# Two engines in turn for the PSUM copies of the last two softmax chains in an FFT and soft mixture-of-experts kernel

## The chip, the cores and the metric

The kernel runs on one core of one Trainium2 chip. The metric is the device time of one execution in microseconds (us). The engines of a core run side by side, each through its own queue of instructions in order: TensorE (PE in the profile: the matmuls and transposes; PEld: its weight loads), VectorE (DVE), ScalarE (ACT), GpSimd (POOL) and SyncE (SP, which here only issues transfers). TensorE writes its results into PSUM tiles; VectorE or ScalarE copies them from there into SBUF, where TensorE can read them again.

## What is computed

```python
X = np.fft.rfft(x, axis=1)                         # x: 8 x 2496 x 256
y = np.fft.irfft(X * (filt_r + 1j * filt_i)[None], n=2496, axis=1)
x = y.reshape(19968, 256)
logits = x @ phi                                   # 32 slots, 4 for each of 8 experts
d = softmax over the 19968 rows of logits (axis 0)
slot_input = d.T @ x                               # 32 x 256
slot_out[e] = relu(slot_input[e] @ w1[e]) @ w2[e]  # hidden size 1024
c = softmax over the 32 slots of logits (axis 1)
out = c @ slot_out                                 # 19968 x 256
```

## The kernel before

Each of the 8 batches goes through a Fourier transform that is written as two layers of matmuls with a round trip through DRAM between them (`s1_unit`, lines 305 to 312, then `x_unit`, line 339). `x_unit` also multiplies by the filter on VectorE (lines 352 and 353) and adds on VectorE and GpSimd (355, 356). `t_unit` transposes the spectrum (366), copies it to a `y` tile (368), and makes the logits of the spectrum (377, copied to `lt` at 384). One slot of the main loop does one `x_unit` and one `t_unit`; there are ten slots to a batch.

The softmax over the rows needs logits in the time domain. That is done group by group in the generator `chain(g)`. `GROUPS` puts batches 0 and 1, 2 and 3, and 4 and 5 together; group 3 is batch 6 alone, and group 4 is batch 7 alone. The text calls them chain 3 and chain 4: they are "the last two". With one batch in a group, `nb` is 1, `R` is 64 and `SA` is 8, and a chain has these steps. In each, TensorE fills a PSUM tile and one engine copies it:

- `lsb` (transposes at 410): two tiles, of 512 and of 128 columns, copied by VectorE at 411.
- `v1` (matmuls at 423): three tiles of 7, 7 and 6 values of t, copied by ScalarE at 430.
- `v` (transposes at 443): two tiles of 512 and 192 columns, copied by VectorE at 444.
- `lg`, the logits in the time domain (450): two tiles, each read twice, first by a maximum on VectorE (451), then by a copy on ScalarE (457). The maximum over partitions follows in small steps (464, 467, 469, 471, 474, 476).
- `d`: subtract the maximum on VectorE (488), exponential on ScalarE (489), in three pieces.
- `u`, the forward transform of `d` (506): three PSUM tiles of shape [128, 2, 24, 10], that is, 480 floats or 1920 bytes in each partition. Each is copied in two halves, h = 0 and h = 1, by ScalarE at 516: 240 and 240 columns twice, then 180 and 140.
- `u2` (transposes at 523): two tiles of 512 and 128 columns, copied by VectorE at 524.
- `dt` (537): two tiles of 512 and 128 columns, copied by ScalarE at 544.
- `dd` (transposes at 553): two tiles of 512 and 128 columns, copied by VectorE at 554.
- `z` and `s`: the sum and the weighted sum of the rows (561 and 581), added into `s_run` (571 and 591).
- Last the softmax over slots, which only the output needs: `rm` (602), the subtraction (604), the exponential (605), the sum `r_all` (607) and its reciprocal (609, 610).

Chain 3 takes its PSUM tiles from one pool of two; chain 4 takes turns between two such pools, which the other work has left by then.

After the last slot, a loop advances chain 4 and chain 3 in turn until both are done. When they are, the slot inputs are formed (804), the expert network runs (816 to 842) and the output is computed (859 to 912) and written. The weights of the expert network are loaded by SP into buffers as these come free; the last 24 of the 64 weight loads (issued at line 736) go into `y` tiles, which come free when `s` of chain 3, and then `s` of chain 4, has read them, and for four of them when the first layer of the network has read the weights that lie there.

The order in which each engine gets its instructions is not the order of the program text alone. The kernel is built with `schedule_with_timeline_sim=True`: a planner orders the instructions of each engine by a simulated time before the kernel is built, and that order is then fixed. It also sets all waits between engines. In the trace it can be seen that `rm` of chain 3 (602) stands ahead of `mx` (469) of the same chain, which the program text has long before it.

A plain float matmul shows as two rows in the trace, a transpose as one.

Of the kernel before, what the change touches and what calls it, by code (L numbers as in the profile page):

```python
# [39 lines left out]
NG = len(GROUPS)  # L40
NSPILL = 2
OUT_ORDER = (4, 5, 0, 1, 2, 3, 6, 7)
P = 128
# [176 lines left out]
def fft_soft_moe(ctx, tc, x, fr, fi, fny, phi, w1, w2, cst, w1q, bmat, out):  # L220
    nc = tc.nc
    pe, dve, act, pool_e, sp = nc.tensor, nc.vector, nc.scalar, nc.gpsimd, nc.sync
# [26 lines left out]
    def C(name, lo=0, hi=None):  # L249
        o, rows, cols = OFF[name]  # L250
        hi = cols if hi is None else hi
        return cst_t[0:rows, o + lo : o + hi]
# [137 lines left out]
    def chain(g):  # L390
# [5 lines left out]
        def psum(shape, name):  # L396
            pool, tag = banks[turn[0] % len(banks)]
            turn[0] += 1
            return pool.tile(shape, F32, tag=tag, name=name)

        nb = len(bs)
        R = nb * 64
        lsb = wk.tile([P, nb, NT, SLOTS], F32, tag="cc", name=f"lsb_{g}", bufs=1)
        for b2, b in enumerate(bs):
            lf = lsb[:, b2].rearrange("k t e -> k (t e)")
            for i0 in (0, 4):
                pl = psum([P, 4, P], f"ltr_{b}_{i0}")
                n = min(4, 5 - i0)
                for i in range(n):
                    pe.transpose(pl[:, i, :], lts[b][:, i0 + i, :], ident)  # L410
                dve.tensor_copy(
                    lf[:, i0 * P : (i0 + n) * P], pl.rearrange("k i q -> k (i q)")[:, 0 : n * P]
                )
            yield
        v1 = wk.tile([P, KP // 2, 2, NT], F32, tag="ca", name=f"v1_{g}", bufs=1)
        for t0 in range(0, NT, 7):
            n = min(7, NT - t0)
            pv = psum([P, 7, KP // 2, 2], f"v1_{g}_{t0}")
            for t in range(t0, t0 + n):
                for b2 in range(nb):  # L420
                    for h in range(2):
                        q = (b2 * 2 + h) * 32
                        pe.matmul(  # L423
                            pv[q : q + 32, t - t0].rearrange("q k r -> q (k r)"),
                            lsb[:, b2, t, :],
                            minv_t[:, t, h * KP : (h + 1) * KP],
                            start=True,
                            stop=True,
                        )
            act.copy(v1[0:R, :, :, t0 : t0 + n], pv[0:R, 0:n].rearrange("q t k r -> q k r t"))  # L430
            yield
        v = wk.tile([QP, NH, R], F32, tag="cb", name=f"v_{g}", bufs=1)
        lg_t = lgp.tile([KR, NH, nb, 2, SLOTS], F32, tag=f"lg{max(g, NSPILL)}", name=f"lg_{g}")
# [3 lines left out]
        v1f = v1.rearrange("q k r t -> q (k r t)")  # L437
        SA = 512 // R
        for s0 in range(0, NH, SA):
            n = min(SA, NH - s0)  # L440
            pv = psum([QP, SA, R], f"v_{g}_{s0}")
            for s in range(n):
                pe.transpose(pv[:, s, :], v1f[0:R, (s0 + s) * QP : (s0 + s + 1) * QP], ident[0:R, 0:R])
            dve.tensor_copy(v[:, s0 : s0 + n, :], pv[:, 0:n])
            if s0 != SA or nb == 1:
                yield
        for s0 in range(0, NH, SA):
            n = min(SA, NH - s0)
            pv = psum([KR, SA, R], f"lg_{g}_{s0}")
            pe.matmul(pv[:, 0:n], C("cq"), v[:, s0 : s0 + n, :], start=True, stop=True)  # L450
            dve.tensor_reduce(
                out=cm[:, s0 // SA, :],
# [29 lines left out]
        u = wk.tile([P, HT, 2 * N2], F32, tag="ca", name=f"u_{g}", bufs=1)  # L482
        mbc = m_new[0:KR].rearrange("s (o e) -> s o e", o=1)

        def dispatch(a0):
            x0, x1 = 2 * nb * a0, 2 * nb * min(a0 + 4, NH)
            mb = mbc.broadcast_to([KR, x1 - x0, SLOTS])
            dve.tensor_tensor(out=d[:, x0:x1], in0=lgf[:, x0:x1], in1=mb, op=ALU.subtract)
            act.activation(d[:, x0:x1], d[:, x0:x1], AF.Exp)
# [3 lines left out]
        for a0 in range(0, NH, 4):  # L493
            n = min(4, NH - a0)
            if a0 + 4 < NH:
                dispatch(a0 + 4)
            pu = psum([P, 2, 4 * PK * 2, HT], f"u_{g}_{a0}")
            for h in range(2):
                for a in range(a0, a0 + n):
                    i = h * NH + a  # L500
                    kr, jn = (KR, PK) if i < NI - 1 else (N1, 1)
                    r0 = (a - a0) * 2 * PK
                    for b2 in range(nb):
                        for th in range(2):
                            q = (b2 * 2 + th) * 32
                            pe.matmul(
                                pu[q : q + 32, h, r0 : r0 + 2 * jn].rearrange("q r t -> q (r t)"),
                                dv[0:kr, a, b2, h, :],
                                C("w1d", th * PK * NT, th * PK * NT + jn * NT)[0:kr],
                                start=True,  # L510
                                stop=True,
                            )
            for h in range(2):
                k0 = (h * NH + a0) * PK * 2
                nk = min((h * NH + a0 + n) * PK, N2) * 2 - k0
                act.copy(u[0:R, :, k0 : k0 + nk], pu[0:R, h, 0:nk].rearrange("q r t -> q t r"))
            yield
        u2 = wk.tile([P, HT, nb, 2, SLOTS], F32, tag="cc", name=f"u2_{g}", bufs=1)
        for t0 in range(0, HT, SA):
            n = min(SA, HT - t0)  # L520
            pu = psum([P, SA, R], f"u2_{g}_{t0}")
            for t in range(n):
                pe.transpose(pu[:, t, :], u[0:R, t0 + t, :], ident[0:R, 0:R])
            dve.tensor_copy(u2[:, t0 : t0 + n].rearrange("k t b h e -> k t (b h e)"), pu[:, 0:n])
            if t0 != 0:
                yield
        NR = NT // 4
        dt = wk.tile([P, nb * NR, P], F32, tag="ca", name=f"dt_{g}", bufs=1)
        for r0 in range(0, nb * NR, 4):
            n = min(4, nb * NR - r0)  # L530
            pd = psum([P, 4, P], f"dt_{g}_{r0}")
            for r in range(r0, r0 + n):
                b2, tr = divmod(r, NR)
                for j in range(4):
                    t = 4 * tr + j
                    th, ti = divmod(t, HT)
                    pe.matmul(  # L537
                        pd[32 * j : 32 * j + 32, r - r0, :],
                        u2[:, ti, b2, th, :],
                        C("bh") if t == 0 else b_t[:, t, :],  # L540
                        start=True,
                        stop=True,
                    )
            act.copy(dt[:, r0 : r0 + n], pd[:, 0:n])
            if r0 != 4:
                yield
        dd = wk.tile([P, nb, NT, SLOTS], F32, tag="cb", name=f"dd_{g}", bufs=1)
        ddf = dd.rearrange("k b t e -> k (b t e)")
        for r0 in range(0, nb * NR, 4):
            n = min(4, nb * NR - r0)  # L550
            pd = psum([P, 4, P], f"dd_{g}_{r0}")
            for r in range(n):
                pe.transpose(pd[:, r, :], dt[:, r0 + r, :], ident)
            dve.tensor_copy(ddf[:, r0 * P : (r0 + n) * P], pd.rearrange("k r q -> k (r q)")[:, 0 : n * P])
            if r0 != 0:
                yield

# [6 lines left out]
        if g > 0:  # L564
# [7 lines left out]
                out=s_run[:, DIM:], in0=s_run[:, DIM:], scalar=alc, in1=pz, op0=ALU.mult, op1=ALU.add  # L572
# [17 lines left out]
        if g > 0:  # L590
            dve.scalar_tensor_tensor(
                out=s_run[:, 0:DIM], in0=s_run[:, 0:DIM], scalar=alc, in1=pss, op0=ALU.mult, op1=ALU.add
# [158 lines left out]
    for n in range(NS + LT):  # L751
# [20 lines left out]
        if n >= LT:  # L772
            b, c = divmod(n - LT, CPB)
# [141 lines left out]
    for b in OUT_ORDER:  # L915
        st = tail.tile([P, 2, SQ], F32R, tag="st", name=f"st_{b}", bufs=SB)
        t0 = b * SEQ
# [45 lines left out]
```

## Time and profile before

| what | value |
|---|---|
| median of 3 runs | 431.23 us (430.06 to 432.34) |
| the profiled execution | 425.78 us, of which 423.9 us are its span |
| TensorE busy | 374.5 us (88%) |
| VectorE busy | 269.8 us (64%) |
| ScalarE busy | 218.6 us (52%) |
| mean granted clock of TensorE | 0.944 of 2.4 GHz |

A share of busy time is a mean over stages with different limits. The change touches only the stretch between about 301 us and 339 us of the span, so the views of that stretch count. In a row of the windows view, each engine has its busy time and, in brackets, its number of instructions; then come the granted clock of TensorE as a share of 2.4 GHz, the mean busy share of the 16 DMA engines (it can be a little over 1), and the GB/s. In a row of the timeline, the first number is the start, the second the duration, and a row with "x2" holds two instructions of a kind back to back; what stands in brackets at the end is the idle time of the engine before it and who ended it.

### The profile page before, as it was taken

Reading aid. Unit: us, or ns where it says so; the run is one execution under the profiler, and the core shown is the slowest. Engines: PE = TensorE matmul, PEld = TensorE weight load, DVE = VectorE, ACT = ScalarE, POOL = GpSimd, SP = SyncE. Lnnn points to the kernel's source line nnn. Section 1 sums busy time; section 2 is a strip of 40 time slices with the busy share of each in tenths; the row PEclk is TensorE's granted clock in tenths of the full one; section 3 lists DMA queues with packets and bytes.
Section 4 is the critical chain, followed back from the end, with each engine's and each line's share of the span. In section 5 each row is a group of like instructions: output and inputs, shape, how many; then the busy total and the mean of one; then the engine's idle time right before and its main releaser. Section 6 shows DMA issues by size and latency. Waiting matters only on the chain.

```text
span 423.9 us, 12672 instructions
## 1 busy us (share of the span) xinstructions
PE 374.5 (88%) x5065; PEld 291.3 (69%) x5065; DVE 269.8 (64%) x496; ACT 218.6 (52%) x475; POOL 201.9 (48%) x234
## 2 busy tenths in 40 slices
PE   7557998999999999999989999989998799999740
PEld 2225876788877787886867688778767435898730
DVE  1341764886989955878998387896378322787330
ACT  2465666676677656765792333461446121675320
POOL 0027778797768655965966056572200401750000
PEclk9688999999999999999999999999998999999555
DMA  8999999999889686978996524333199895699994
GB/s 209 238 306 288 331 321 327 334 294 344 246 262 337 213 264 206 289 214 256 269 280 167 186 82 121 101 103 101 55 344 347 268 275 185 249 394 381 386 362 166
DMA packets 61820, 107.07 MB, mean 253 GB/s; under 512 B 6142, under 2 KB 37758, under 8 KB 60226
## 3 DMA queue, kind: packets, MB, share of 16 engines
q1 hardware_dynamic: 61762, 106.26, 79.3%
q8 instruction: 40, 0.66, 0.6%
q14 instruction: 18, 0.15, 0.1%
HBM read 63.50 MB, written 42.74 MB: 251 GB/s over the span
## 4 chain that ended last, share of the span: by engine, by line
PE 61%; DMA 16%; DVE 12%; ACT 3%; issue 2%; SPq 2%; POOL 0%; ACTq 0%; DVEq 0%
PE x L339 15%; PE s L308 8%; PE t L366 6%; DMA out<-obr 6%; DMA xt<-in_x 6%; PE s L581 4%; PE l L377 4%; PE out L903 3%; PE v L423 3%; PE dt L537 2%; DMA ash<-a_dram 2%; DVE t L353 2%; PE o L833 2%; PE lg L450 2%; PE s L305 2%
## 5 line engine op out<-in xcount | busy, mean ns | idle before, releaser
L295 POOL TENSOR_TENSOR xl<-xt,xh 117x512 fp32r<-117x512 f32 x77 | 103.0, 1350 | 52.7 <-ACT xh L294 49.9
L339 PE MATMUL x<-b_t,ash 128*128 128x128 f32 x640 | 91.5, 284 | 6.1 <-DMA ash<-a_dram 3.1
L339 PEld LDWEIGHTS x<-b_t,ash 128*128 128x128 f32 x640 | 81.2, 194 | 17.0 <-issue 5.0
L356 POOL TENSOR_TENSOR yt<-yt,t 128x256 f32<-128x256 f32 x80 | 65.9, 826 | 40.7 <-DVE t L353 30.5
L352 DVE TENSOR_TENSOR yt<-x,fr_t 128x512 f32<-128x512 f32 x80 | 54.7, 684 | 39.9 <-PE x L339 36.9
L294 ACT CAST xh<-xt 117x512 fp32r<-117x512 f32 x77 | 46.8, 622 | 35.4 <-DMA xt<-in_x 12.1
L368 ACT COPY y<-t 128x512 f32<-128x512 f32 x80 | 46.5, 591 | 34.3 <-PE t L366 28.6
L312 ACT COPY at<-s 120x512 f32<-120x512 f32 x83 | 48.4, 587 | 21.7 <-PE s L305 8.6
L353 DVE TENSOR_TENSOR t<-x,fi_t 128x512 f32<-128x512 f32 x80 | 54.3, 678 | 0.0
L366 PE MATMUL t<-cst_t,yt 128*128 128x128 f32 x320 | 48.5, 276 | 0.7 <-POOL yt L356 0.4
L355 DVE TENSOR_TENSOR yt<-yt,t 128x256 f32<-128x256 f32 x60 | 43.3, 730 | 0.8
L366 PEld LDWEIGHTS t<-cst_t,yt 128*128 128x128 f32 x320 | 37.3, 141 | 7.9 <-issue 3.1
L308 PE MATMUL s<-xh,w1h 117*120 117x512 f32 x77 | 36.0, 468 | 6.5 <-ACT xh L294 5.5
L903 PE MATMUL out<-so_h,st 32*128 32x256 f32 (+1 forms) x320 | 36.3, 329 | 3.3 <-ACT obr L912 2.4
L903 PE MATMUL out<-so_l,st 32*128 32x256 f32 (+1 forms) x320 | 34.4, 311 | 0.0
L903 PEld LDWEIGHTS out<-so_h,st 32*128 32x128 f32 (+1 forms) x320 | 29.9, 206 | 6.5 <-ACT obr L912 3.0
L308 PE MATMUL s<-xl,w1h 117*120 117x512 f32 x77 | 32.2, 419 | 0.3 <-POOL xl L295 0.2
L308 PE MATMUL s<-xh,w1l 117*120 117x512 f32 x77 | 31.1, 404 | 0.0
L355 POOL TENSOR_TENSOR yt<-yt,t 128x256 f32<-128x256 f32 x20 | 16.2, 811 | 30.5 <-DVE t L353 24.2
L903 PEld LDWEIGHTS out<-so_l,st 32*128 32x128 f32 (+1 forms) x320 | 30.3, 209 | 0.0
L377 PE MATMUL l<-yt,phi_t 128*32 128x128 f32 x640 | 26.1, 278 | 0.9 <-ACT y L368 0.7
L912 DVE COPY ob<-out 128x512 f32<-128x512 f32 x32 | 20.6, 684 | 7.6 <-PE out L903 7.3
(118 smaller groups left out, 552.6 us busy)
## 6 DMA issues: line engine op xcount, KB each, us to landing
ash<-a_dram SPq DMA_DIRECT2D x80, 256.0 KB
a_dram<-at SPq DMA_DIRECT2D x80, 240.0 KB
xt<-in_x SPq DMA_DIRECT2D x40, 448.0 KB
w<-in_w SPq DMA_DIRECT2D x64, 256.0 KB
out<-ob SPq DMA_DIRECT2D x12, 1024.0 KB
out<-ob SPq DMA_DIRECT2D x8, 512.0 KB
out<-obr SPq DMA_DIRECT2D x8, 448.0 KB
xt<-in_x SPq DMA_DIRECT2D x8, 224.0 KB
```

Of the source, the lines that this page charges most:

```text
L294: act.copy(xh, xs)
L295: pool_e.tensor_tensor(out=xl, in0=xs, in1=xh.bitcast(F32), op=ALU.subtract)
L308: pe.matmul(ps, w, xx, start=(n == 0), stop=(n == 2))
L312: act.copy(at, ps)
L339: pe.matmul(ps[:, 2 * k + dh].rearrange("q r c -> q (r c)"), ash[:, k, dh * P : (dh + 1) * P], b_t[:, t0 + k, :], start=True, stop=True,)
L352: dve.tensor_tensor(out=yt, in0=ps, in1=frv, op=ALU.mult)
L353: dve.tensor_tensor(out=t2, in0=ps[:, :, ::-1, :], in1=fiv, op=ALU.mult)
L355: add.tensor_tensor(out=yt[:, :, 1, :], in0=yt[:, :, 1, :], in1=t2[:, :, 1, :], op=ALU.add)
L356: pool_e.tensor_tensor(out=yt[:, :, 0, :], in0=yt[:, :, 0, :], in1=t2[:, :, 0, :], op=ALU.subtract)
L366: pe.transpose(pt[:, k, dh, :], yt[:, c % 2, 2 * k + dh].rearrange("q r c -> q (r c)"), ident)
L368: act.copy(y, pt.rearrange("k p h d -> k p (h d)"))
L903: nc.tensor.matmul(prs[k][0:rows, mm, :], st[q, n // 2, c0 : c0 + rows], (so_h, so_l)[n % 2][q, :], start=(n == 0), stop=(n == 3),)
```

## The change

A helper `evac` takes the place of the copies at lines 411, 430, 444, 516, 524, 544 and 554. It gets the engine that made the copy before. For chains 0 to 2 it uses that engine. For chains 3 and 4 it counts the copies into each output tile: the first, third and fifth go to that engine, the second, fourth and sixth to the other one.

```diff
+        turns = {}
+
+        def evac(first, out, src):
+
+            n = turns[out.tensor.name] = turns.get(out.tensor.name, -1) + 1
+            if (first is dve) == (g < NG - 2 or n % 2 == 0):
+                dve.tensor_copy(out, src)
+            else:
+                act.copy(out, src)
+
...
-                dve.tensor_copy(
-                    lf[:, i0 * P : (i0 + n) * P], pl.rearrange("k i q -> k (i q)")[:, 0 : n * P]
-                )
+                evac(dve, lf[:, i0 * P : (i0 + n) * P], pl.rearrange("k i q -> k (i q)")[:, 0 : n * P])
...
-            act.copy(v1[0:R, :, :, t0 : t0 + n], pv[0:R, 0:n].rearrange("q t k r -> q k r t"))
+            evac(act, v1[0:R, :, :, t0 : t0 + n], pv[0:R, 0:n].rearrange("q t k r -> q k r t"))
...
-            dve.tensor_copy(v[:, s0 : s0 + n, :], pv[:, 0:n])
+            evac(dve, v[:, s0 : s0 + n, :], pv[:, 0:n])
...
-                act.copy(u[0:R, :, k0 : k0 + nk], pu[0:R, h, 0:nk].rearrange("q r t -> q t r"))
+                evac(act, u[0:R, :, k0 : k0 + nk], pu[0:R, h, 0:nk].rearrange("q r t -> q t r"))
...
-            dve.tensor_copy(u2[:, t0 : t0 + n].rearrange("k t b h e -> k t (b h e)"), pu[:, 0:n])
+            evac(dve, u2[:, t0 : t0 + n].rearrange("k t b h e -> k t (b h e)"), pu[:, 0:n])
...
-            act.copy(dt[:, r0 : r0 + n], pd[:, 0:n])
+            evac(act, dt[:, r0 : r0 + n], pd[:, 0:n])
...
-            dve.tensor_copy(ddf[:, r0 * P : (r0 + n) * P], pd.rearrange("k r q -> k (r q)")[:, 0 : n * P])
+            evac(dve, ddf[:, r0 * P : (r0 + n) * P], pd.rearrange("k r q -> k (r q)")[:, 0 : n * P])
```

In each of the two chains, VectorE takes over the second `v1` tile, the half h = 1 of all three `u` tiles and the second `dt` tile; ScalarE takes over the second tile of `lsb`, `v`, `u2` and `dd`.

## Rows read from the trace of the kernel before

**Rows 1.** The windows view, from the start of chain 3 to the end of the expert network (columns as above).

```profile
301.00:307.20 6.20, 6.20 (x135) 5.23 (x132) 3.77 (x7) 3.31 (x7) 2.79 (x4) 1.00 0.25 90
307.20:314.10 6.90, 6.51 (x119) 4.82 (x118) 4.19 (x11) 3.87 (x9) 0.00 (x0) 1.00 0.98 314
314.10:318.00 3.90, 3.62 (x57) 2.72 (x59) 3.32 (x11) 1.45 (x5) 0.00 (x0) 1.00 1.06 391
318.00:322.20 4.20, 3.10 (x73) 2.47 (x67) 4.20 (x16) 2.63 (x10) 0.00 (x0) 1.00 1.06 385
322.20:331.80 9.60, 9.60 (x191) 7.75 (x191) 5.68 (x19) 4.24 (x14) 0.57 (x1) 0.82 0.80 257
331.80:339.00 7.20, 4.52 (x94) 2.84 (x93) 2.94 (x9) 0.75 (x2) 4.22 (x12) 1.00 1.04 331
339.00:360.00 21.00, 20.20 (x227) 9.36 (x228) 4.60 (x9) 3.50 (x7) 1.24 (x2) 1.00 0.81 233
```

**Rows 2.** The chain of work that ended last, in order of time, from 314.82 us on: start, us, what.

```profile
314.82 0.96 DVE v L444 x2
315.78 0.11 DVE m_run L476
...
321.44 0.69 DVE u L524
...
331.71 0.70 DVE u L524
...
332.46 1.40 PE dt L537 x40
...
333.88 0.59 ACT dt L544
...
335.21 0.70 DVE dd L554
...
335.96 0.24 PE z L561 x8
```

**Rows 3.** Groups of VectorE instructions by line and shape between 301 and 339 us: names, shapes, count, busy us, mean ns of one, idle before.

```profile
L451 DVE TENSOR_REDUCE cm<-lg 117x32 f32<-117x512 f32 x2 | 1.4, 687 | 1.7 <-PE lg L450 1.7
L444 DVE COPY v<-v 120x512 f32<-120x512 f32 x2 | 1.4, 692 | 0.9 <-PE v L443 0.9
L444 DVE COPY v<-v 120x192 f32<-120x192 f32 x2 | 0.7, 347 | 0.0
L411 DVE COPY lsb<-ltr 128x128 f32<-128x128 f32 x2 | 0.6, 280 | 0.0
```

**Rows 4.** The same view for ScalarE.

```profile
L516 ACT COPY u<-u 64x240 f32<-64x240 f32 x8 | 2.4, 354 | 1.4 <-PE u L506 1.4
L516 ACT COPY u<-u 64x140 f32<-64x140 f32 x2 | 0.6, 280 | 0.0
```

**Rows 5.** The timeline of VectorE and ScalarE where both read the first `lg` tile of chain 3.

```profile
311.17 1.11 DVE L451 TENSOR_REDUCE cm<-lg 117x32 f32<-117x512 f32 x2 [1.74 <-PE lg L450]
311.90 0.81 ACT L457 COPY lg<-lg 117x512 f32<-117x512 f32 x2 [1.28 <-DVE cm L451]
```

**Rows 6.** The timeline of VectorE from 317.56 us on: the first and the last of each of the softmax over slots of chain 3.

```profile
317.56 0.52 DVE L604 TENSOR_TENSOR lg<-lg,rm 117x352 f32<-117x352 f32 x1
...
318.80 0.51 DVE L602 TENSOR_REDUCE rm<-lg 117x11 f32<-117x352 f32 x1
...
320.30 0.51 DVE L607 TENSOR_REDUCE r_all<-lg 117x11 f32<-117x352 f32 x1
```

**Rows 7.** The timeline of ScalarE around the `u` copies of both chains, and that of TensorE behind the ones of chain 3.

```profile
318.16 0.61 ACT L516 COPY u<-u 64x240 f32<-64x240 f32 x2
318.66 0.50 ACT L605 ACTIVATE lg<-lg 117x352 f32<-117x352 f32 x1
319.06 0.31 ACT L457 COPY lg<-lg 117x192 f32<-117x192 f32 x1
...
319.65 0.98 ACT L516 COPY u<-u 64x240 f32<-64x240 f32 x4
...
320.69 0.83 PE L523 MATMUL u<-cst_t,u 64*128 64x64 f32 x10 [0.77 <-ACT u L516]
...
328.02 1.19 ACT L516 COPY u<-u 64x240 f32<-64x240 f32 x4 [1.40 <-PE u L506]
```

**Rows 8.** From the chain of work again: `dt` and the first `u` of chain 4, and the end of `s` of chain 3 with `u2` of chain 4 behind it.

```profile
322.18 2.36 PE dt L537 x40
324.53 1.73 PE u L506 x42
...
327.55 1.13 PE u L506 x34
...
328.85 2.19 PE s L581 x40
331.04 0.66 PE u L523 x8
```

**Rows 9.** The windows view by microsecond (columns as in the first group).

```profile
320.00:321.00 1.00, 0.31 (x5) 0.32 (x6) 1.00 (x4) 0.63 (x4) 0.00 (x0) 1.00 1.05 381
...
323.00:324.00 1.00, 1.00 (x28) 0.99 (x21) 1.00 (x5) 0.67 (x2) 0.00 (x0) 0.50 1.03 354
```

**Rows 10.** The waits between 339 and 375 us: who waited for whom, us in total, times, longest; the one line in which TensorE waits for a weight load.

```profile
PEld o L833 <- DMA w<-in_w: 0.3, 1, 0.3
```

## The prediction

> **What bounds the kernel now.** I read the windows view first, cut at the steps of chains 3 and 4 [rows 1], because busy shares over the whole span mix stages with different limits. The reader is to see that the bound moves from one engine to another within 38 us. From 301 to 307.2 us TensorE is busy for 6.20 of 6.20 us, up to 314.1 for 6.51 of 6.90: there the last slots of the main loop, chain 3 and the start of chain 4 fill it together. From 314.1 to 318 and on to 322.2 us TensorE idles for 0.28 and 1.10 us, and VectorE is busy for 3.32 of 3.90 and then for 4.20 of 4.20 us: it is the bound. From 322.2 to 331.8 TensorE is full again (9.60 of 9.60). From 331.8 to 339 nothing is full: only chain 4 is left, and each step waits for the one before. From 339 on the expert network keeps TensorE busy for 20.20 of 21.00 us.
>
> Then the chain of work that ended last [rows 2]. From 314.82 us to the end of the `u2` copy that starts at 321.44 us it runs through VectorE instructions alone, which confirms the windows. From 331.71 us on it alternates between a TensorE step and one copy.
>
> What is saved or lost in this stretch reaches the end. The expert network starts when `s` of chain 4 is done, TensorE is busy in it almost without a gap [rows 1], and it waited for a weight only once, for 0.3 us [rows 10]. A loss therefore passes through in full. A gain does so only if chain 3 shares in it, since many of the last weight loads wait for the `y` tiles that `s` of chain 3 frees.
>
> **The change part by part.** First the prices of one copy. VectorE: 280 ns for 128 columns, 347 for 192, 692 for 512 [rows 3]; that is 1.08 ns a column ((692-347)/320), so by estimate 0.40 us for 240 columns, 0.29 for 140 and 0.64 for 462. The `u` copy reads with a stride, and no strided copy on VectorE is shown; the strided maximum of 512 columns took 687 ns, no more than the plain copy's 692 [rows 3], so I take no surcharge. ScalarE: 354 ns for 240 columns and 280 for 140 [rows 4]. In a chain, VectorE thus takes over 0.64 + 0.40 + 0.40 + 0.29 + 0.28 = 2.0 us and gives away 0.28 + 0.35 + 0.28 + 0.28 = 1.2 us. The change gives net work, 0.8 us a chain, to the busier of the two engines. What it costs depends on where it lies.
>
> *The second copies of `lsb`, and `v1` (301 to 314 us).* TensorE is full, so quicker copies only let it take its work in another order: 0. The `v1` tile of chain 4 that moves (the second of three) is followed by a third which ends last and stays on ScalarE: 0. Bounds: a gain of 0.5 us, if that third copy was held up by the second on ScalarE all along, and a loss of 0.3, if VectorE takes the second copy just ahead of the small steps of chain 3's maximum.
>
> *The second copy of `v`, chain 4.* Here it counts. Both copies stand in the chain of work (0.96 us for the pair), and `m_run` of chain 3 is queued behind them [rows 2]. A copy costs its queue some 0.09 us less than its duration, as consecutive instructions overlap: 0.692 + 0.347 - 0.96 = 0.08. So taking the second away saves 0.347 - 0.09 = 0.26 us of the VectorE-bound stretch.
>
> *The `u` copies of chain 3.* The half h = 1 of three tiles moves to VectorE in exactly the stretch where it is full: 0.40 + 0.40 + 0.29, less 0.09 each, is 0.82 us. ScalarE gets free earlier, and `u2` waited 0.77 us for its last `u` copy [rows 7], but this is no gain: the `u2` copy, chain 4's maximum and its `d` all queue on VectorE. Behind the waiting h = 1 copy in its queue stand `cm`, `cmax`, `mx` and `dg` of chain 4.
>
> The two halves are meant to run side by side, but they are halves of one PSUM tile. What the trace shows for two engines that read one PSUM tile is the first `lg` tile: ScalarE's copy at 311.90 us had waited 1.28 us and was released by VectorE's maximum, which needs nothing from the copy [rows 5]. So I expect the h = 1 copy to wait for the h = 0 copy. The Trainium skill, "PSUM — Partial Sum Buffer", section "PSUM bank collisions raise a hardware error", says that ScalarE and VectorE must not read one bank in the same 32-partition quadrant at once, and that the compiler's scheduler adds a dependency even between two reads. By that rule the wait is there, as in the row. Were the halves free to overlap, the sum below would stay as it is, since the queue of VectorE is the limit and not the pair. The wait is what the slower rival is made of.
>
> Bounds of this part: 0, if the planner lets chain 3's softmax over slots fall back (six instructions, 604, 602 and 607, of 0.5 us each, which only the output needs, stand in this very stretch [rows 6]); and 0.82 plus the stalls priced below.
>
> *The `u` copies of chain 4 (326 to 329.3 us).* Taken at 0: the last four end at 328.02 + 1.19 = 329.21 us [rows 7], and `u2` starts at 331.04, when `s` of chain 3 is off TensorE [rows 8]. A serial pair ends perhaps 0.1 us later; the cover is 1.8 us. Without it, the pairs would cost some 0.1 us each.
>
> *The second copies of `u2`, `dt` and `dd`.* Taken at 0: in the chain of work each of these steps holds one copy, the long first one (0.70, 0.59, 0.70 us), and the step behind it starts within 0.06 us of its end [rows 2]. The short one, of 128 columns, already runs under the next step. This is the stretch in which the kernel waits most visibly for copies, and the change doesn't shorten the ones it waits for.
>
> **Sum.** -0.26 + 0.82 = +0.56 us. No transfer or queue of SP is moved, except as the `y` tiles come free later. On the profiled execution's 425.78 us this makes 426.3; that execution is 5.45 us below the median of the runs, so I put the difference on the median: 431.2 + 0.6 = 431.8 us. This kernel's runs can tell about 0.5% from no change, which is 2.2 us, so the forecast is "the same".
>
> **The rivals.**
>
> *Faster: chain 3 gets through sooner, and the clock stays up.* TensorE was busy for 0.31 us of the microsecond from 320 us, waiting for the `u` copies; by 323 us the granted clock was 0.50, the lower level of 1.2 GHz [rows 9]. `dt` of chain 3 took 2.36 us there [rows 8], the same 40 matmuls of chain 4 took 1.40 at full clock [rows 2]; and the 42 `u` matmuls behind it took 1.73 where 34 took 1.13 [rows 8], so 1.40 for 42. If halving ScalarE's part of the `u` copies closes this gap, the clock gives back 0.96 + 0.33 = 1.3 us; with the 0.26 of `v`, and the 0.82 hidden because the planner puts off chain 3's softmax, that is 429.7 us. If the new order also puts `u2` of chain 4 ahead of `s` of chain 3, whose 2.19 us [rows 8] would then cover chain 4's copies, it is about 427.5. For it: TensorE's wait there is for exactly these copies, and the planner may order anew from 301 us on. Against it: VectorE has no free time in this stretch to take the halves. Chance 0.22, of which 0.13 for over 0.5%.
>
> *Slower: VectorE's queue stalls on ScalarE's.* An h = 1 copy that stands in VectorE's queue before ScalarE has come to h = 0 holds everything behind it. Ahead of the h = 0 copies ScalarE has exponentials of 0.50 us and an `lg` copy of 0.31 [rows 7]; with the h = 0 copy of 0.35 a stall can be up to 1.2 us a tile. Two such stalls and the 0.82 of work make 3.2 us, less 0.26: 434.1 us. It decides from the point where the stalls add up to 1.6 us beyond the sum above. For it: ScalarE is without a gap there too. Against it: the planner sees the wait, and may put other work ahead. The longer gap on TensorE would also lengthen the time at the low clock, by up to a microsecond. Chance 0.20, of which 0.15 for over 0.5%.
>
> *The change doesn't do what it says.* For `u` that is part of the forecast: the halves follow one another. For `u2`, `dt` and `dd` too: they are in turn, but the second copy was covered. If this holds for all of it, the time is 431.2 us. It is within the forecast's chance.
>
> **How the numbers follow.** The forecast, from -0.5 to +1.6 us around no change, has 0.58; the rivals have 0.22 and 0.20. Faster by over 0.5% 0.13, within 0.5% 0.72, slower 0.15. The range takes in most of the two rivals: from the clock's gain (-1.6, and part of the way to the new order), 429.2, to the stalls, 434.0.
>
> **What would show it.** Right: in the windows from 318 to the `dt` of chain 3, VectorE full, with three `u` copies in it, each starting where a ScalarE copy of the same line ends; `dt` of chain 3 starting some 0.6 us later; the single long copies between 331 and 339 us unchanged. Wrong: a granted clock of 1.00 through `dt` of chain 3, `u2` of chain 4 ahead of `s` of chain 3, the two halves of a `u` tile at the same time, or VectorE idle behind ScalarE for over 1.6 us. A difference of over 1 us outside the stretch from 301 us on would be outside all of this.

## The result, and the profile after

| | before | after |
|---|---|---|
| median of 20 runs each | 429.61 us (425.20 to 432.88) | 430.68 us (427.23 to 435.33) |
| ratio after / before, run beside each other | | 1.0075, 95% interval 1.005 to 1.010 |
| profiled execution, its span | 425.78, 423.9 us | 431.24, 429.5 us |
| mean granted clock of TensorE | 0.944 | 0.939 |

The change makes the kernel slower, by 0.0075 x 429.6 = 3.2 us (2.1 to 4.3). (The ratio compares undisturbed runs made side by side; the two medians take in all runs, and lie 1.1 us apart.) The time lies within the range on record; the forecast of +0.6 us does not fit the interval. That it lies in the range is in part luck: the range was put around 431.2 us, the median of three runs, and over twenty runs the kernel before came out 1.6 us lower. A loss of 3.2 us on 431.2 would have been 434.4, just above the range's 434.0. In the profile after, a line number of the chains is 8 higher than before, and every copy that the change touches has line 409 (VectorE) or 411 (ScalarE).

The two profiled executions differ by more than the 3.2 us. One part of that is no effect of the change: chain 3 begins at 301.09 us of the span before and at 302.00 after, and in the other profiled executions anywhere between 300.9 and 307.3 us, behind the same instructions in the same order on every engine. So from here on I measure two pieces. The *stretch* runs from the first `ltr` transpose of chain 3 to the start of `psi`, the first matmul behind both chains. The *network* runs from `psi` to `so_h`, where the expert network ends. The stretch took 37.93 us before and 41.34 after, the network 20.41 and 20.35.

The windows view of the kernel after, cut at the same steps as the first six of [rows 1], with the same columns:

```profile
302.00:308.10 6.10, 6.10 (x135) 5.21 (x132) 4.20 (x7) 2.84 (x7) 2.79 (x4) 1.00 0.31 94
308.10:315.00 6.90, 6.50 (x120) 4.94 (x118) 3.82 (x8) 3.81 (x10) 0.00 (x0) 1.00 0.91 284
315.00:318.80 3.80, 3.72 (x62) 2.78 (x64) 3.71 (x13) 1.97 (x7) 0.00 (x0) 1.00 1.06 389
318.80:324.40 5.60, 3.52 (x65) 2.85 (x60) 4.72 (x17) 2.08 (x7) 0.00 (x0) 0.86 1.06 384
324.40:333.00 8.60, 8.60 (x161) 7.00 (x163) 5.16 (x17) 3.03 (x9) 0.00 (x0) 0.70 0.70 221
333.00:343.30 10.30, 7.49 (x133) 5.14 (x125) 4.05 (x11) 1.78 (x5) 4.77 (x12) 0.83 0.94 289
```

Up to `m_run` nothing is lost. The fourth row is longer than its counterpart by 1.4 us, and TensorE idles in it for 2.08 us instead of 1.10. The fifth is shorter by 1.0 us, and the sixth longer by 3.1. The granted clock, which was below 1.00 in one stage of [rows 1], is below it in three.

The chain of work of the kernel after, which answers to [rows 2] and [rows 8]:

```profile
315.70 0.69 DVE v L409
316.39 0.11 DVE m_run L484
...
319.92 0.30 DVE u L409
...
321.72 0.31 DVE u L409
...
322.30 0.22 DVE u L409
...
322.56 1.18 PE u L531 x10
...
324.40 2.36 PE dt L545 x40
...
330.85 2.19 PE s L589 x38
333.04 0.83 PE u L514 x26
333.89 0.31 ACT u L411
334.22 0.31 DVE u L409
...
334.58 0.73 PE u L531 x8
...
336.07 1.65 PE dt L545 x32
```

Two things are new. The `u` copies of VectorE stand in the chain. And behind `s` of chain 3 the chain does not go on with `u2` of chain 4, as at 331.04 us in [rows 8]: the planner has put the last `u` tile of chain 4 behind `s`, and its matmuls and its pair of copies come one after the other with nothing beside them, from 333.04 until `u2` starts at 334.58 us.

The timelines of the kernel after, first ScalarE and VectorE at the three `u` tiles of chain 3 and at the last one of chain 4, then TensorE:

```profile
318.86 0.34 ACT L411 COPY u<-u 64x240 f32<-64x240 f32 x1
...
319.96 0.35 ACT L411 COPY u<-u 64x240 f32<-64x240 f32 x1
321.22 0.30 ACT L411 COPY u<-u 64x180 f32<-64x180 f32 x1 [0.91 <-PE u L514]
...
319.83 0.39 DVE L409 COPY u<-u 64x240 f32<-64x240 f32 x1
...
320.37 0.50 DVE L615 TENSOR_REDUCE r_all<-lg 117x11 f32<-117x352 f32 x1
320.80 0.93 DVE L610 TENSOR_REDUCE rm<-lg 117x11 f32<-117x352 f32 x2
321.65 0.39 DVE L409 COPY u<-u 64x240 f32<-64x240 f32 x1
...
322.23 0.28 DVE L409 COPY u<-u 64x140 f32<-64x140 f32 x1
...
334.22 0.30 DVE L409 COPY u<-u 64x140 f32<-64x140 f32 x1 [0.24 <-ACT u L411]
...
320.28 0.89 PE L514 MATMUL u<-cst_t,d 117*32 117x60 f32 x24 [0.79 <-DVE u L409]
...
322.56 1.18 PE L531 MATMUL u<-cst_t,u 64*128 64x64 f32 x10 [1.19 <-DVE u L409]
```

ScalarE is done with its halves at 319.20, 320.31 and 321.52 us; VectorE comes to the other halves at 319.83, 321.65 and 322.23, in all 2.7 us later, because its queue is full: ahead of the second, for one, stand `r_all` and two `rm` (0.50 us, and 0.93 for the two). TensorE waits twice for that. The third `u` tile of chain 3 can't begin until the first one's PSUM tile is copied (0.79 us), since this chain has two such tiles, and `u2` waits for the last half (1.19 us). Before, there was one wait, of 0.77 us [rows 7].

The windows view of the kernel after by microsecond, columns as above, which answers to [rows 9]:

```profile
319.00:320.00 1.00, 0.49 (x20) 0.34 (x14) 1.00 (x4) 1.00 (x4) 0.00 (x0) 1.00 1.03 379
...
321.00:322.00 1.00, 0.38 (x5) 0.16 (x5) 1.00 (x4) 0.30 (x1) 0.00 (x0) 1.00 1.06 387
...
325.00:326.00 1.00, 1.00 (x28) 1.00 (x23) 1.00 (x4) 0.92 (x4) 0.00 (x0) 0.50 1.08 358
...
328.00:329.00 1.00, 1.00 (x8) 0.72 (x4) 0.32 (x2) 0.00 (x0) 0.00 (x0) 0.50 0.99 314
...
337.00:338.00 1.00, 1.00 (x24) 0.67 (x15) 0.00 (x0) 0.26 (x1) 1.00 (x5) 0.50 0.88 241
```

The clock is at its lower level, 1.2 GHz, from 322.8 to 329.6 and again from 336.5 to 339.9 us; before, only from 322.2 to 325.7. I call this the *low time*. Over the whole stretch, from windows of half a microsecond, it is 3.4 us before and 10.2 after.

### The profile page after: what moved, and what is told of

Its sections match the earlier page's. It is cut to its first block, busy times and chain, and to the rows that moved or that the text cites. A ratio compares the mean times of both kernels' runs of the same rounds, so it can differ in the third digit from the quotient of the medians.

```text
span 429.5 us, 12672 instructions
## 1 busy us (share of the span) xinstructions
PE 376.8 (88%) x5065; PEld 292.8 (68%) x5065; DVE 272.1 (63%) x498; ACT 217.7 (51%) x473; POOL 201.7 (47%) x234
## 4 chain that ended last, share of the span: by engine, by line
PE 61%; DMA 18%; DVE 9%; ACT 3%; issue 2%; SPq 2%; POOL 0%; DVEq 0%; POOLq 0%; ACTq 0%
PE x L339 14%; PE s L308 9%; DMA xt<-in_x 8%; DMA out<-obr 7%; PE t L366 6%; PE s L589 4%; PE l L377 4%; PE out L911 4%; PE v L431 3%; PE dt L545 3%; DMA ash<-a_dram 2%; PE lg L458 2%; PE o L841 2%; PE h L824 2%; DVE t L353 2%
## 5 line engine op out<-in xcount | busy, mean ns | idle before, releaser
L911 PE MATMUL out<-so_h,st 32*128 32x256 f32 (+1 forms) x320 | 34.6, 311 | 5.4 <-ACT obr L920 4.3
L911 PEld LDWEIGHTS out<-so_h,st 32*128 32x128 f32 (+1 forms) x320 | 27.8, 191 | 8.5 <-ACT obr L920 4.9
L911 PE MATMUL out<-so_l,st 32*128 32x256 f32 (+1 forms) x320 | 32.1, 294 | 0.0
L911 PEld LDWEIGHTS out<-so_l,st 32*128 32x128 f32 (+1 forms) x320 | 27.8, 192 | 0.0
```

What stands on the lines that cost most here:

```text
L911: nc.tensor.matmul(prs[k][0:rows, mm, :], st[q, n // 2, c0 : c0 + rows], (so_h, so_l)[n % 2][q, :], start=(n == 0), stop=(n == 3),)
```

## The experiments

Theory A: the loss is the low clock, which TensorE's new waits bring about. Theory B: it is the net work on VectorE, +0.8 us or more in chain 3. Theory C: it is the new order of TensorE, with the last `u` tile of chain 4 behind `s` of chain 3. The table holds the two kernels and all twelve runs, in us: stretch, low time in it, start of `dt` of chain 3 after the start of the stretch, network, and the ratio to the kernel before where it was timed.

| run | stretch | low | `dt` | network | ratio (95%) |
|---|---|---|---|---|---|
| before | 37.93 | 3.4 | 21.09 | 20.41 | |
| r1_before | 37.77 | 3.4 | 21.09 | 21.79 | |
| after | 41.34 | 10.2 | 22.40 | 20.35 | 1.0075 (1.005 to 1.010) |
| r2_after | 41.51 | 10.2 | 22.50 | 20.36 | |
| e1_u_only | 41.59 | 6.8 | 22.28 | 20.35 | 1.0131 (1.0062 to 1.0199) |
| e2_all_but_u | 35.49 | 0.0 | 20.82 | 23.01 | 0.9997 (0.9955 to 1.0040) |
| e11_u_chain4 | 36.92 | 3.4 | 20.83 | 22.48 | 0.9966 (0.9923 to 1.0009) |
| e4_s_held | 39.66 | 6.8 | 22.30 | 22.64 | 1.0070 (1.0029 to 1.0110) |
| e5_u_behind_s | 38.42 | 3.4 | 21.09 | 21.74 | 1.0048 (0.9990 to 1.0106) |
| e6_rows_late | 38.54 | 0.0 | 23.71 | 20.35 | 1.0047 (1.0014 to 1.0081) |
| e8_fill | 36.74 | 0.0 | 22.10 | 22.28 | 1.0042 (0.9995 to 1.0089) |
| e12_fill_before | 37.44 | 0.0 | 22.14 | 20.36 | 1.0032 (0.9995 to 1.0070) |
| e9_best | 35.23 | 0.0 | 22.26 | 22.71 | 0.9999 (0.9960 to 1.0038) |
| e10_cl_late | 35.88 | 3.4 | 23.57 | 20.36 | 0.9945 (0.9907 to 0.9982) |

**Both kernels once more** (r1_before, r2_after, unchanged), to see what one profiled execution is worth.

> The kernel before, profiled once more, to see what of the stretch (37.86 us from the first ltr transpose of chain 3 to psi, with a granted clock of 0.50 during dt of chain 3) belongs to the kernel. If the fall of the clock belongs to the kernel: 37.7 to 38.1 us, the clock at 0.50 in dt of chain 3 again. If it belongs to the execution: dt of chain 3 in about 1.4 us, stretch 36.3 to 36.8 us.

> The changed kernel, profiled once more. If its two falls of the clock belong to the kernel: stretch 41.1 to 41.6 us, about 10 us of it at a granted clock of 0.50. If they belong to the execution: 37.5 to 40 us.

The stretch came back within 0.17 us for both, and the low time at 3.4 and 10.2. The network of the kernel before took 1.4 us more this time, with a wait of 1.6 us for weights where [rows 10] has 0.3. Stretch and network together are thus 58.3 and 59.6 us before, 61.7 and 61.9 after. The difference of the means, 2.8 us, agrees with the 3.2 of the timed runs. By the stretch alone it is 3.6 us: where weights are waited for anyhow, a part of the loss is covered.

**Only `u`, and all but `u`.** The condition in `evac` is cut in two:

```diff
-            if (first is dve) == (g < NG - 2 or n % 2 == 0):
+            u_tile = out.tensor.name.startswith(f"u_{g}")
+            if (first is dve) == (g < NG - 2 or n % 2 == 0 or not u_tile):
```

This is e1; in e2 the last term is `or u_tile`.

> Only the u halves of chains 3 and 4 are copied by two engines; all other copies as before. The stretch from the first ltr transpose of chain 3 to the psi matmul is 37.9 us in the kernel before and 41.3 in the changed one. Theory (the u halves carry the whole loss): 40.5 to 41.8 us, ratio to before about 1.007; dt of chain 3 starts 22 us after the first transpose or later. Rival (the other copies do it, by the order that they bring): 37.9 to 38.5 us, ratio 1.000.

> All copies of chains 3 and 4 in turn but those of u, which stay on ScalarE. Theory (the u halves carry the whole loss): the stretch takes 37.3 to 38.0 us (0.3 us less for the second copy of v), ratio 0.998 to 1.001. Rival (the other copies): 40 to 41.3 us, ratio 1.005 or more.

With `u` alone the stretch is as long as with the whole change; without it, it is 2.4 us shorter than before, and the intervals of the two ratios lie apart. So the loss is in the `u` copies.

But e1 does not lose it in the way that after does. From its timeline of TensorE:

```profile
322.66 0.83 PE L532 MATMUL u<-cst_t,u 64*128 64x64 f32 x10 [1.19 <-DVE u L410]
...
324.29 1.16 PE L546 MATMUL dt<-b_t,u 128*32 128x128 f32 x35
...
329.36 0.24 PE L570 MATMUL z<-cst_t,dd 128*32 128x1 f32 x8 [0.72 <-DVE dd L410]
...
338.74 4.09 PE L590 MATMUL s<-y,dd 128*32 128x256 f32 x40
```

TensorE waits 1.19 us ahead of `u2` of chain 3, as in after, and yet the clock stays at 1.00 and `dt` of chain 3 is done in 1.30 us. The clock falls only at 335.5 us, where just chain 4 is left, and `s` of chain 4 takes 4.09 us instead of 2.35.

e2's clock did not fall at all, which I had not expected. A row of its chain of work:

```profile
324.32 1.30 PE dt L546 x40
```

and from its waits the one of TensorE for weights (us in total, times, longest):

```profile
PEld o L842 <- DMA w<-in_w: 2.6, 6, 0.6
```

`dt` of chain 3 takes 1.30 us instead of 2.36. But the gain ends in a wait for weights, 2.6 us, and the ratio is 0.9997.

**The order of TensorE back (e4, on the kernel after).** `z` and `s` of chain 3 are held until chain 4 has issued its last `u` tile:

```diff
+        if g == NG - 1:
+            passed.add("u")
         u2 = wk.tile([P, HT, nb, 2, SLOTS], F32, tag="cc", name=f"u2_{g}", bufs=1)
...
+        while g == NG - 2 and "u" not in passed:
+            yield
         pz = psum([P, 1], f"z_{g}")
```

> The changed kernel, but the program lets chain 3 pause ahead of z until chain 4 has issued u, so that the last u tile of chain 4 stands ahead of s of chain 3 on TensorE, as in the kernel before; nothing else moves. Theory (1.5 us of the loss is the last u tile of chain 4 behind s, which lays its two serial copies open): stretch 39.5 to 40.0 us, u2 of chain 4 starts right behind s. Rival (the low clock is the whole of it, the order only moves work): 40.8 to 41.5 us.

The chain of work of e4:

```profile
326.58 2.36 PE dt L548 x40
...
334.05 2.19 PE s L594 x40
336.24 0.65 PE u L534 x8
...
337.66 1.12 PE dt L548 x32
```

`u2` of chain 4 again starts as `s` ends, `dt` of chain 4 takes 1.12 us instead of 1.65, and the second fall of the clock is gone. The stretch gets 1.68 us shorter, as the theory had it, though not for the order alone: up to `u2` of chain 4 the gain is 0.69 us, and the other 0.99 us come behind it, where the second fall was. The first fall stays, and the gain goes into a wait of 2.2 us for weights.

**The new order alone (e5, on the kernel before).** An order edge without a wait puts the last `u` tile of chain 4 behind `s` of chain 3:

```diff
+                            if g == NG - 1 and a0 == 8:
+                                info = mybir.DependencyInfo(mybir.DependencyClass.NoSync, mybir.DependencyReason.DATA)
+                                tc.add_manual_dep(i.ins, passed[NG - 2].ins.name, info, reason="u behind s")
```

> The kernel before with all its engines, but the last u tile of chain 4 is put behind s of chain 3 on TensorE by an order edge, as the changed kernel has it; nothing else moves in the stretch. Theory (this order alone costs the 26 matmuls and the two copies that s no longer covers): u2 of chain 4 starts 1.3 to 1.5 us later, stretch 39.1 to 39.4 us where the clock is as before. Rival (the copies were the cost, the order costs nothing): 37.9 us.

This is not what was expected. The chain of work shows why:

```profile
327.73 2.28 PE s L585 x40
330.01 0.71 PE u L507 x24
330.75 0.48 ACT u L520 x2
```

The `u` matmuls stand behind `s`, but `s` moved up by as much; only the copies lie open. The order alone costs 38.42 - 37.93 = 0.49 us, with the same low time.

**TensorE's waits filled (e8 on the kernel after, e12 on the kernel before).** Behind each exponential of chain 3's softmax over slots stand four matmuls of 128 x 128 whose result nobody reads; the second half of them is ordered behind the third `u` tile, so that they run where TensorE would wait:

```diff
+                for k in range(4):
+                    i = pe.matmul(fill[:, k % 4], row[:, 0:P], row[:, 0:P], start=True, stop=True)
+                    if x0 > 0:
+                        info = mybir.DependencyInfo(mybir.DependencyClass.NoSync, mybir.DependencyReason.DATA)
+                        tc.add_manual_dep(i.ins, passed[g, 8].ins.name, info, reason="fill")
```

> The changed kernel with eight 128-column matmuls that nobody reads, on finished rows of lg of chain 3: four ahead of its last u tile and four behind it, in TensorE's two gaps. The last u tile of chain 4 then stands ahead of s of chain 3 by itself, as in e4. Theory (the gaps let the clock fall, and that is a part of the loss of its own): the clock stays at 1.00 through dt of chain 3, which takes 1.3 to 1.5 us, stretch 37.3 to 38.5 us. Rival (the gaps have nothing to do with the clock): it falls as in e4, stretch 39.3 to 40 us.

> The kernel before with the eight matmuls of e8 that nobody reads, in TensorE's gap ahead of u2 of chain 3; nothing else moves but small steps of VectorE. Theory (the gap lets the clock fall in the kernel before as well, at a price of 1.3 us): clock 1.00 through dt of chain 3, which takes 1.3 to 1.5 us in place of 2.36, stretch 36.3 to 36.9 us. Rival (it falls regardless): 37.7 to 38.1 us.

The chain of work of e8:

```profile
327.02 1.30 PE dt L546 x40
...
331.76 2.19 PE s L590 x40
333.95 0.65 PE u L532 x8
```

and of e12:

```profile
325.46 1.30 PE dt L538 x40
```

With this useless work the changed kernel's stretch is 4.6 us shorter: the clock stays at 1.00, and in the planner's new order `u2` is right behind `s`. Compared with e4, which has that order too, 6.8 us of low time are gone for 39.66 - 36.74 = 2.92 us, 0.43 us for each. In e12 the fills hold `dt` up by 1.05 us, more than I expected, and the stretch is still 0.49 us shorter; so 3.4 us of low time are worth 1.54, or 0.45 each. The Trainium skill, "TensorE: Matmul & The Clock Gate", section "Terms", puts the penalty at the throttled time times one minus the share of the clock that is left, which by estimate is 0.50 us for each. The runs show a little less: 0.43 and 0.45 in chain 3, and 0.29 at the second fall in after (0.99 us for 3.4), where each step waits for a copy.

The timed runs don't confirm the gain. e12's stretch and network together are 57.8 us against 58.3 and 59.6 before, but its ratio is 1.0032 (0.9995 to 1.0070); e8's is 1.0042, with a wait of 2.0 us for weights.

**VectorE's optional work put off (e6, on the kernel after; e9 the same on e2).** The softmax over slots of chain 3 is ordered behind the `d` of chain 4, and in the program chain 3 pauses ahead of it until chain 4 has come to `s`, so that the `u` halves find VectorE free. The order edge is:

```diff
+            if g == NG - 2:
+                info = mybir.DependencyInfo(mybir.DependencyClass.NoSync, mybir.DependencyReason.DATA)
+                tc.add_manual_dep(i.ins, passed["d"].ins.name, info, reason="rows late")
```

> The changed kernel, but the softmax over slots of chain 3 (rm, subtraction, exponential, r_all) is held back by an order on VectorE until d of chain 4 has been subtracted. Theory (VectorE's queue is the limit of the stretch up to dt of chain 3): dt of chain 3 starts 20.5 to 21.3 us after the first transpose in place of 22.3, u of chain 4 comes ahead of s of chain 3 by itself, stretch 37.5 to 39 us. Rival (the serial pairs of u copies are the limit, whatever else VectorE does): dt starts at 22 us or later, stretch 40.5 or more.

> All copies of chains 3 and 4 in turn but those of u (as e2), and the softmax over slots of chain 3 held back on VectorE until d of chain 4 is subtracted (as e6). u2 of chain 4 then stands ahead of s of chain 3. Theory (VectorE's queue is the limit, and s can cover the u2 copy): stretch 33.3 to 34.8 us, ratio to before 0.990 to 0.997. Rival (what is gained comes back as a wait for the weights or in the output): stretch as said, ratio 0.998 to 1.002.

In e6 the clock never fell and the stretch is as expected, though `dt` of chain 3 came later than expected (23.71 us): the planner used the room to put chain 4's `u` ahead of it. This does not part A from B, since VectorE's queue got shorter and the low time went, both at once. It does show that waits are not enough for a fall: TensorE waits 0.85, 0.49, 0.84 and 1.03 us between the `u` and the `dd` of chain 3, and the clock stays at 1.00. In the timed runs e6 is slower than before (1.0047), which the stretch and the network, 58.9 us together, do not explain. e9 has the shortest stretch of all, and no gain: 2.2 us wait for weights.

**`u` in turn in chain 4 alone (e11)**: e2, with the halves of chain 4 in turn.

> As e2 (all copies of chains 3 and 4 in turn but those of u), and in addition the u halves of chain 4, not those of chain 3. Theory (the pairs cost where VectorE is full, in chain 3; those of chain 4 are covered by s of chain 3): stretch 35.3 to 35.9 us as in e2 (35.5), clock 1.00 throughout. Rival (every serial pair costs, in chain 4 as well): 36.5 us or more.

```profile
322.03 2.36 PE dt L546 x40
```

`dt` of chain 3 starts as in e2 (20.83 and 20.82 us), but it takes 2.36 us, as the clock falls for 3.4 us. The stretch is in the rival's range, but not for its reason. Up to 20.4 us the two versions run the same instructions, each started within 0.02 us of its time in the other, on all four compute engines; the clock falls at 20.46 us, and the first copy that differs comes later. The 1.43 us between the two stretches is 3.4 x 0.42, so no cost of the copies themselves is seen in chain 4. The timed runs agree (0.9966), and their median of 427.82 us is below the profiled execution's 429.89. Why the clock fell here and not in e2 is open.

**The loads of `cl` behind the weights (e10, on e9).** The planner had two loads of `cl`, the spilled logits of groups 0 and 1, which only the output needs, ahead of the last 14 weight loads:

```diff
-        sp.dma_start(lgs[g], c_dram[g])
+        i = sp.dma_start(lgs[g], c_dram[g])
+        info = mybir.DependencyInfo(mybir.DependencyClass.NoSync, mybir.DependencyReason.DATA)
+        tc.add_manual_dep(i.ins, last_w[0].ins.name, info, reason="cl behind w")
```

> As e9, but the two loads of cl (the spilled logits of groups 0 and 1, which the output needs late) are put behind the last 14 weight loads in SP's queue; every engine's order is that of e9. Theory (the 2.4 us that e9 gains up to psi came back as a wait for weights of 2.5 us, behind these loads): TensorE waits for weights under 0.7 us, psi to so_h takes 20.4 to 21 us, ratio to before 0.990 to 0.997. Rival (the output's transfers set the end whatever comes before): ratio 0.998 to 1.002.

SP's queue in e9, in its timeline, and then its row of TensorE's waits for weights:

```profile
335.21 1.10 SPq L814 DMA_DIRECT2D cl<-c_dram  x2
```

```profile
PEld o L852 <- DMA w<-in_w: 2.2, 5, 0.6
```

and the same in e10:

```profile
326.11 24.67 SPq L756 DMA_DIRECT2D w<-in_w  x30
351.11 1.11 SPq L815 DMA_DIRECT2D cl<-c_dram  x2
```

```profile
PEld h L838 <- DMA w<-in_w: 0.6, 2, 0.3
```

The network goes from 22.71 to 20.36 us, and this is the one version that beats the kernel before: 0.9945 (0.9907 to 0.9982), 2.4 us. Its interval overlaps that of e9 (0.9960 to 1.0038), so the step from e9 alone is shown by the wait and not by the time. Its clock fell for 3.4 us in the profiled execution (430.42 us, where the median of its runs is 426.02); in e9, with the same order on the compute engines in the stretch, it did not.

## Why the prediction was right or wrong

**The cause.** The loss lies in the `u` halves that VectorE copies: e1 has all of it, e2 none of it. How it comes about is read by cutting the stretch at three steps of TensorE, the starts of `u2` of chain 3, of `u2` of chain 4 and of `z` of chain 4 (us, rounded; the low time of the piece in brackets):

| run | up to `u2`, chain 3 | up to `u2`, chain 4 | up to `z`, chain 4 | up to `psi` |
|---|---|---|---|---|
| before | 19.60 | 10.28 (3.4) | 4.99 | 3.06 |
| after | 20.56 | 12.01 (6.8) | 5.71 (3.4) | 3.06 |
| e4_s_held | 20.57 | 11.32 (6.8) | 4.72 | 3.06 |
| e8_fill | 20.52 | 8.44 | 4.72 | 3.06 |
| e12_fill_before | 20.65 | 8.75 | 5.00 | 3.06 |
| e2_all_but_u | 19.24 | 8.42 | 4.78 | 3.06 |
| e1_u_only | 20.79 | 10.37 | 5.58 (3.1) | 4.85 (3.7) |

The stretch grew by 3.41 us. Of this, 0.96 us is there at `u2` of chain 3, before the clock falls: the wait for VectorE's queue (B). The first fall costs 11.32 - 8.44 = 2.88 us (e4 against e8), the second 5.71 - 4.72 = 0.99, and the one that the kernel before has cost it 10.28 - 8.75 = 1.53; so the clock makes 2.34 us (A). The last `u` tile behind `s` costs 12.01 - 11.32 = 0.69 (C). The other copies in turn give back 8.75 - 8.44 = 0.31 and 4.99 - 4.72 = 0.27. These prices rest on one profiled execution of each version, two of before and after.

In e1 the parts are others. Against before it loses 1.19 us up to `u2` of chain 3 and 10.37 - 8.75 = 1.62 in the second piece at full clock; its low time costs 2.38 in the last two pieces, and it doesn't have the 1.53 of before. There the clock is 0.85 us of 3.66, and waits and order are the rest. So A is the largest part in after, but not in every version with the halves on VectorE.

**The step that failed.** The sum put one term at nothing, the clock, and that term is two thirds of the result. The prediction had the fall of the clock before it in [rows 9], priced a gain from it (-1.3 us) in the faster rival, and in the slower rival gave a longer low time "up to a microsecond" as a remark, while the sum took the low time as unchanged. The low time measured 10.2 us instead of 3.4. What the sum lacked is this step: work put on the engine that TensorE waits for makes TensorE's wait longer (0.77 us before, 0.79 and 1.19 after), and in before and after alike the clock falls behind that wait, at 322.2 and 322.8 us. Without the clock the account makes +1.07 us, where the sum had +0.56.

**Point by point.**

- *The second copies of `lsb` and `v1` at nothing*: right as far as seen; the first two rows of the windows have TensorE busy for 6.10 and 6.50 us against 6.20 and 6.51 [rows 1].
- *The second copy of `v`, -0.26 us*: right, a little small. `m_run` of chain 3 comes 14.31 us after the start of the stretch instead of 14.61, and `u2` of e2, which has no `u` in turn, 0.36 earlier.
- *The prices of the `u` halves*, 0.40, 0.40 and 0.29: measured 0.39, 0.39 and 0.28.
- *The pair is serial*: right where it can be seen. At the last tile of chain 4 ScalarE's half ends at 334.19 and VectorE's begins at 334.22. In chain 3 none of the halves starts where ScalarE's ends, as I had said it would; the queue of VectorE is later still.
- *The `u` copies of chain 3, +0.82 us, and `dt` some 0.6 us later*: `dt` was 1.31 later. `u2` starts 0.96 us later (20.56 instead of 19.60 after the start), against a forecast of 0.56, and 1.32 later than in e2, against 0.82: the wait for the PSUM tile of the first `u` was not in the sum. From there to `dt` another 0.35 is lost to the clock, which here falls as early as `u2`.
- *The `u` copies of chain 4 at nothing, "the cover is 1.8 us"*: no cost is seen where the cover stands (e11), but in after it does not stand. The planner took it away by putting the last `u` tile behind `s`. By e5 that costs 0.49 us; by e4 against after 0.69, and 1.68 together with the second fall of the clock, which e4 does not have.
- *The second copies of `u2`, `dt` and `dd` at nothing*: on the safe side. At full clock the pieces behind `u2` of chain 3 take 8.75 and 5.00 us with the old engines (e12), 8.42 and 4.78 in e2, 8.44 and 4.72 in e8. So they give some 0.3 us in each, though the prediction took the short copy as covered.
- *The slower rival*: its mechanism did not happen. VectorE is busy for 3.71 of 3.80 us and then for 4.72 of 5.60, idle only behind the last `u` copy; it never stood behind a ScalarE half in chain 3. Its size, 434.1 - 431.2 = 2.9 us, came about in another way than the one named; that it is near the measured 3.2 is luck.
- *The faster rival*: its condition, a clock that stays up, was met by e2, e6, e8 and e9, up to chain 4 by e1 too, but not by the change itself.
- *A loss passes in full, a gain only in part*: right for the gain, and stronger than put: in e2, e4, e8 and e9 TensorE waited 2.0 to 2.6 us for weights, which took most of what the stretch gave, or all; e10 shows what held the weights. For the loss, right against the first profile of before: the 3.4 us went through to `so_h`. Against r1_before, which waits 1.6 us for weights itself, a part of it is covered.

**B and C** are not refuted: 0.96 and 0.69 us, of which the other copies give back 0.58. With `u` alone in turn (e1), they outweigh the clock.

**What stays open.** When the clock falls, and so how much of the 3.2 us of the timed runs it makes. In the stretch it fell in both profiled executions of each kernel, and with TensorE's waits filled (e8, e12) it fell in neither; so it is likely that the waits have to do with it. But they don't settle it. The row of e2's windows where TensorE waits for the `u` copies:

```profile
322.00:323.00 1.00, 0.35 (x5) 0.27 (x5) 1.00 (x4) 0.68 (x4) 0.00 (x0) 1.00 1.05 387
```

It is nearly as idle as before (0.31 [rows 9]), and the clock stays at 1.00. e1 and e6 have waits as long, and it stays there too. e2 and e11, and e9 and e10, run the same instructions at the same times up to where it falls in one and not in the other. And ahead of the stretch, where all fourteen profiled executions run the same instructions in the same order, the low time is anything from 10.2 to 23.9 us (13.7 in before, 23.9 in r1_before). So one program's executions differ in it, and two of each kernel don't tell how often the stretch falls as in the profiles. In e10 the same 3.4 us of low time lengthened the stretch by only 0.65 us against e9, so 0.43 to 0.45 is not the price everywhere either. Open too is why e6, e8 and e12 are no faster than before in the timed runs, though their stretch and network together (58.9, 59.0 and 57.8 us) are within or below the 58.3 and 59.6 us of before. Not tried: PSUM tiles of their own for the two halves, which would take the pair apart.

## What to carry to other kernels

Before work moves to an engine, see who waits for that engine and what TensorE does in that wait: 0.96 us more of waiting came with 2.3 us lost to the clock in after, and 1.19 us with 0.85 in e1, and the sum needs a line for that. Here the tile of a split copy was free only when the later of the two queues had come to it, so the price was that queue's backlog (up to 1.3 us), not the copy (0.4). And where a gain does not reach the end, look for the next wait: here two loads of no urgency stood ahead of the weights on SP.

## What the runs showed of the hardware that was not expected

Eight matmuls of 128 x 128 that nobody reads made a stretch 2.9 us shorter (e8 against e4, which has the same order around `s`); `dt` went from 2.36 to 1.30 us. The granted clock can part two executions that have run the same instructions at the same times, to within 0.02 us on all compute engines, up to the point where it falls: 3.4 us of low time in e11 and none in e2. The Trainium skill, "TensorE: Matmul & The Clock Gate", section "A second HAM failure mode: psum-queue depth-cycling", tells of a kernel in which short idle times of TensorE between groups of matmuls, at its PSUM buffers, made the clock swing between its levels. The trace after agrees, with waits of 0.79 and 1.19 us for PSUM copies ahead of the fall at 322.8 us; e1, with waits of 0.76 and 1.19 us at the same place and no fall there, shows that such waits alone don't decide it.
